# Moving 24 elementwise products from VectorE to GpSimd, decay rows to SyncE's queue, and v loads ahead of k, in a gated linear-attention and GEGLU kernel

## The chip, the cores and the metric

The kernel runs on one core of a Trainium2 chip. The metric is the device time of one execution in microseconds (us); lower is better. In the profiles PE is TensorE (PEld its weight loads), DVE is VectorE, ACT is ScalarE, POOL is GpSimd and SP is SyncE; "POOLq" and "SPq" are the queues on which GpSimd and SyncE issue DMA transfers. "L309" is line 309 of the kernel.

## The reference, cut to what matters

For 4 batches, 8 heads, 768 time steps and head size 48, a complex decay `a` is normalised, a state is decayed and updated at each step, and read out by q. The 3072 outputs of width 384 then pass through a gated feed-forward block.

```python
mag = np.sqrt(a_re * a_re + a_im * a_im)
scale = np.minimum(mag, 0.999) / (mag + 1e-06)
a_re_n, a_im_n = (a_re * scale, a_im * scale)
for t in range(S):                       # 768 steps
    new_re = ar * S_re - ai * S_im       # ar, ai: a_re_n, a_im_n at t
    new_im = ar * S_im + ai * S_re
    S_re, S_im = (new_re + k[t] v[t]^T, new_im)
    y[:, :, t] = q[t]^T S_re
...
gelu = 0.5 * g * (1.0 + erf(g * inv_sqrt2))        # g = x @ w_gate
ffn_out = gelu * val @ w_out                       # val = x @ w_val
out = x + ffn_out / (1.0 + np.exp(-(x @ w_res)))
```

## The kernel before

The kernel cuts the 768 steps into groups of 256 (12 groups in all; the tiles are 128 partitions by 768 columns: two blocks of 128 steps, each 8 heads of 48). The decay becomes cumulative sums of log-magnitude and angle. `E` and `Ei` are exp(+) and exp(-) of the first, `CS` holds cosine and sine of the second, and the attention works on `Q = q*E*CS` and `K = k*Ei*CS`. The products q*E and k*Ei are the subject of the change:

```python
def products(g):
    def x0():
        qE = pK.tile([128, W], BF, tag="qE", name="qE")
        nc.vector.tensor_tensor(out=qE, in0=flat(T["q", g]), in1=T["E", g], op=OP.mult)       # L309
        ...
    def x1():
        kE = pK.tile([128, W], BF, tag="kE", name="kE")
        nc.vector.tensor_tensor(out=kE, in0=flat(T["k", g]), in1=T["Ei", g], op=OP.mult)      # L314
        ...
    def mk(nm, src):                                      # Q from qE, K from kE:  L321
        ...  nc.vector.tensor_tensor(out=t, in0=T["CS", g], in1=sb, op=OP.mult)
    return [x0, mk("Q", "qE"), x1, mk("K", "kE")]
```

Other VectorE instructions that play a part below. The first two read two, respectively one, fp32 tile of SBUF (the engines' working memory), the third one int32 tile of SBUF:

```python
nc.vector.scalar_tensor_tensor(out=lm, in0=T["s", g], scalar=0.5, in1=lm, op0=OP.mult, op1=OP.add)   # L197
nc.vector.tensor_scalar(out=lm, in0=lm, scalar1=LNMAX, scalar2=None, op0=OP.min)                     # L198
...
nc.vector.tensor_scalar(out=fg[:, :, 0, :].bitcast(int32), in0=fg[:, :, 1, :].bitcast(int32), ...)   # L246
```

The decay of a whole group goes through DRAM as rows, to be turned into columns `m` and multiplied into `M` on VectorE (L282):

```python
def turn(nm, g, srcs):
    ...
    for i, src in enumerate(srcs):
        nc.gpsimd.dma_start(out=md[i:i + 1, :], in_=src)              # dm<-E, dm<-Ei, dm<-ar
    for u in range(2):
        nc.gpsimd.dma_start(out=m[u * D:(u + 1) * D]..., in_=md...)   # m<-dm
```

Each output block is stored twice: SyncE writes the gated part, then GpSimd adds x with an accumulating store, which has to wait until the first has landed (43.1 us in 13 waits of GpSimd in the kernel before). The v loads are on GpSimd's queue as well, each behind a one-element copy (`landed`) that waits for k's load (53.0 us in 8 waits):

```python
nc.sync.dma_start(out=out[t0:t0 + 128, :], in_=ot)                                                # L470
if u < NU - 1:
    nc.gpsimd.dma_start(out=out[t0:t0 + 128, :], in_=T["x", token(u, jj)], accum_op=OP.add)       # L472
...
for u in range(-1, NU + 1):
    phase_x(u)      # decay of unit u+1, output projection of unit u-1
    ...             # loads of the decays
    phase_y(u)      # gelu block of unit u, products and first attention of unit u+1
    for g in gs(u + 3):
        load_q(g)
        after_landing(T["k", g], call(load_v, g))
```

A unit is two groups but for the first and last. ACT's function table is loaded anew for logarithm and exponential, for arctangent and sine, and for gelu (21 loads of 1.28 us in the trace). That splits the execution: a load stage, then a decay stage and a gelu stage in turn, five times, then a tail. The table loads on ACT mark the borders: a decay stage runs from the load of the logarithm table to that of the gelu table. One more gelu stage stands at the end of the load stage and is counted with it. Stages are numbered below without it, but the expectations count it: their "second gelu stage" is the first of the five here.

Of the kernel before, what the change touches and what calls it, by code (L numbers as in the profile page):

```python
# [12 lines left out]
OP = mybir.AluOpType  # L13
# [3 lines left out]
def weave(*streams):  # L17

    order = []
    for si, (begin, end, steps) in enumerate(streams):  # L20
        n = len(steps)
        for i, step in enumerate(steps):
            order.append((begin + (end - begin) * (i + 0.5) / n, si, i, step))
    for _, _, _, step in sorted(order, key=lambda e: e[:3]):
        step()
# [3 lines left out]
def kernel(  # L29
# [13 lines left out]
    nc = tc.nc  # L43
    B, H, S, D = q.shape
# [47 lines left out]

    lda = ctx.enter_context(tc.tile_pool(name="lda", bufs=6))
    ldq = ctx.enter_context(tc.tile_pool(name="ldq", bufs=4))
    ldv = ctx.enter_context(tc.tile_pool(name="ldv", bufs=6))
    pS = ctx.enter_context(tc.tile_pool(name="pS", bufs=2))
    pE = ctx.enter_context(tc.tile_pool(name="pE", bufs=2))
    pQ = ctx.enter_context(tc.tile_pool(name="pQ", bufs=2))
    pK = ctx.enter_context(tc.tile_pool(name="pK", bufs=1))
    sqp = ctx.enter_context(tc.tile_pool(name="sqp", bufs=2))  # L100
    stt = ctx.enter_context(tc.tile_pool(name="stt", bufs=2))
    mp = ctx.enter_context(tc.tile_pool(name="mp", bufs=3))
    xp = ctx.enter_context(tc.tile_pool(name="xp", bufs=10))
    xtp = ctx.enter_context(tc.tile_pool(name="xtp", bufs=2))
    hb = ctx.enter_context(tc.tile_pool(name="hb", bufs=1))
    ob = ctx.enter_context(tc.tile_pool(name="ob", bufs=2))
# [7 lines left out]
    T = {}  # L114
# [11 lines left out]
    def rows(a, g, c):  # L126
        b, s = divmod(g, NS)
        t0 = (s * C + c) * 128
        return a[b, :, t0:t0 + 128, :].rearrange("h t d -> t h d")


    def load_a(g):
        for nm, src in (("ar", a_re), ("ai", a_im)):
            t = lda.tile([128, C, H, D], FP, tag=nm, name=nm)
            for c in range(C):
                nc.sync.dma_start(out=t[:, c], in_=rows(src, g, c))  # L136
            T[nm, g] = t
        T["a"] = g + 1

    def load_q(g):  # L140
        for nm, src in (("q", q), ("k", k)):
            t = ldq.tile([128, C, H, D], FP, tag=nm, name=nm)
            for c in range(C):
                nc.sync.dma_start(out=t[:, c], in_=rows(src, g, c))  # L144
            T[nm, g] = t

    def load_v(g):
        t = ldv.tile([128, C, H, D], BF, tag="v", name="v")
        for c in range(C):
            nc.gpsimd.dma_start(out=t[:, c], in_=rows(v, g, c))  # L150
        T["v", g] = t
# [16 lines left out]
    def after_landing(t, f):  # L168

        w = singles.tile([1, 1], FP, name="landed%d" % len(T))  # L170
        i = nc.gpsimd.tensor_copy(out=w, in_=t[0:1, C - 1, H - 1, D - 1:D])
        with tc.issue_after(i.ins):
            f()

    def flat(t):
        return t.rearrange("p c h d -> p (c h d)")
# [81 lines left out]
    def turn(nm, g, srcs):  # L258
        n = len(srcs)
        md = dr.tile([n, DM], FP, tag="d" + nm, name="d" + nm)  # L260
        for i, src in enumerate(srcs):
            nc.gpsimd.dma_start(out=md[i:i + 1, :], in_=src)
        m = mp.tile([128, n, H], FP, tag=nm, name=nm)
        for u in range(2):
            nc.gpsimd.dma_start(out=m[u * D:(u + 1) * D].rearrange("p r h -> p (r h)"),
                                in_=md.rearrange("r (h d) -> d (r h)", h=H))
        T[nm, g] = m

    def decay0(g):
        turn("m1", g, [T["lm", g][0:1, 0:DM]])  # L270
# [5 lines left out]
    def decay2(g):  # L276
        turn("m2", g, [T["E", g - 1][127:128, DM:W], T["Ei", g][0:1, 0:DM]])
# [28 lines left out]
    def products(g):  # L306
        def x0():
            qE = pK.tile([128, W], BF, tag="qE", name="qE")
            nc.vector.tensor_tensor(out=qE, in0=flat(T["q", g]), in1=T["E", g], op=OP.mult)  # L309
            T["qE", g] = qE  # L310

        def x1():
            kE = pK.tile([128, W], BF, tag="kE", name="kE")
            nc.vector.tensor_tensor(out=kE, in0=flat(T["k", g]), in1=T["Ei", g], op=OP.mult)  # L314
            T["kE", g] = kE

        def mk(nm, src):
            def x():
                t = pQ.tile([128, C * H, 2, D], BF, tag=nm, name=nm)
                sb = T[src, g].rearrange("p (x u d) -> p x u d", u=1, d=D).to_broadcast([128, C * H, 2, D])  # L320
                nc.vector.tensor_tensor(out=t, in0=T["CS", g], in1=sb, op=OP.mult)  # L321
                T[nm, g] = t
            return x
        return [x0, mk("Q", "qE"), x1, mk("K", "kE")]
# [150 lines left out]
    def table(nm):  # L475
        def f():
            tab(nc.scalar.preload_act_table_set(nm))  # L477
        return f

    def gs(u):  # L480
        return UNITS[u] if 0 <= u < NU else []
# [7 lines left out]
    def call(f, *a):  # L489
        return lambda: f(*a)  # L490
# [4 lines left out]
    def att_steps(u, half):  # L495

        todo = [(g, c, i * C + c) for i, g in enumerate(gs(u)) for c in range(C)]
        n = len(todo) // 2
        steps = []
        for i, (g, c, jj) in enumerate(todo[half * n:half * n + n]):  # L500
            steps += attention(g, c)
            if i > 0:
                steps.insert(-1, call(xt_step, u, jj - 1))
        if n:
            steps.append(call(xt_step, u, half * n + n - 1))
        return steps
# [50 lines left out]
    def phase_y(u):  # L557

        gv = []
        if 0 <= u < NU:  # L560
            table("gelu_and_others")()
            gv = [call(gv_step, u, f) for f in range(KF)]
            rp = [call(rp_step, u, jj) for jj in range(len(gs(u)) * C)]
            gv = gv[:8] + rp[:len(rp) // 2] + gv[8:] + rp[len(rp) // 2:]
        pr = [st for g in gs(u + 1) for st in products(g)]
        weave((0.0, 1.0, gv), (0.0, 0.4, pr), (0.3, 0.95, att_steps(u + 1, 0)))

    def load_first(g):
# [24 lines left out]
    for u in range(-1, NU + 1):  # L593
        phase_x(u)
        while u >= 0 and T["a"] < min(NG, gs(u + 1)[-1] + 6 if gs(u + 1) else NG):
            load_a(T["a"])
        phase_y(u)
        for g in gs(u + 3):
            load_q(g)
            after_landing(T["k", g], call(load_v, g))  # L600


# [28 lines left out]
```

## Time and profile before

Before the change the kernel takes 324.23 us (median of 3 runs, 323.4 to 324.4); the profiled execution spans 322.4 us. The stages, read from the table loads in ACT's timeline:

| stage | length (us) |
|---|---|
| load stage with its gelu stage | 83.5 |
| five decay stages | 17.9, 19.2, 19.6, 17.4, 12.0 (sum 86.1) |
| five gelu stages | 26.4, 26.0, 26.4, 26.3, 23.2 (sum 128.2) |
| tail | 24.6 |

Two lines of the page of the kernel before: busy us by engine (share of the span, instructions), and the chain of work that ended last, by engine:

```profile
PE 272.1 (84%) x2200; PEld 170.5 (53%) x2200; DVE 234.8 (73%) x431; ACT 209.8 (65%) x353; POOL 80.5 (25%) x115
...
PE 56%; SPq 12%; ACT 11%; DMA 9%; DVE 6%; issue 3%; POOL 1%; ACTq 0%; DVEq 0%; POOLq 0%
```

The view of busy time by window shows what a gelu stage is. Here is the fourth gelu stage of the kernel before (start and end, length, then busy time and count of PE, PEld, DVE, ACT, POOL; granted clock; DMA share; GB/s):

```profile
236.33:262.65 26.32, 26.32 (x271) 16.69 (x270) 22.54 (x40) 16.64 (x31) 1.73 (x2) 1.00 0.13 26
```

By the profile PE is busy for all of the 26.32 us: this gelu stage is as long as TensorE's work in it. A decay stage looks different. This is VectorE's timeline early in the second decay stage (127.8 to 147.0) of the kernel before (start, duration, instruction, count, and in brackets the idle time before it and what ended that):

```profile
132.32 1.83 DVE L189 TENSOR_TENSOR ai<-s,ai 128x768 f32<-128x768 f32 x2 [5.11 <-ACT s L124]
...
134.53 0.95 DVE L309 TENSOR_TENSOR qE<-q,E 128x768 bf16<-128x768 f32 x1
...
135.90 0.95 DVE L314 TENSOR_TENSOR kE<-k,Ei 128x768 bf16<-128x768 f32 x1
136.76 1.82 DVE L197 SCALAR_TENSOR_TENSOR ar<-s,ar 128x768 f32<-128x768 f32 x2
138.50 1.05 DVE L198 TENSOR_SCALAR ar<-ar 128x768 f32<-128x768 f32 x2
```

After a wait of 5.11 us for ACT, VectorE runs without a gap, and two products stand in that run. The waits of the kernel before (engine, line, what it waited for; us in total, times, longest), the two lines that the prediction leans on:

```profile
ACT CS L124 <- DVE fg L246: 20.7, 10, 5.2
...
DVE M L282 <- DMA m<-dm: 3.4, 3, 1.6
```

Finally the durations, in the groups of instructions with shapes kept apart (busy us, mean ns of one, idle before):

```profile
L309 DVE TENSOR_TENSOR qE<-q,E 128x768 bf16<-128x768 f32 x12 | 11.4, 950 | 6.8 <-DMA ar<-in_a_re_dram 3.5 <-ACT E L124 3.3
L314 DVE TENSOR_TENSOR kE<-k,Ei 128x768 bf16<-128x768 f32 x12 | 11.4, 946 | 0.0
L197 DVE SCALAR_TENSOR_TENSOR ar<-s,ar 128x768 f32<-128x768 f32 x12 | 11.3, 951 | 3.3 <-ACT s L124 3.3
L198 DVE TENSOR_SCALAR ar<-ar 128x768 f32<-128x768 f32 x12 | 7.0, 594 | 0.0
L246 DVE TENSOR_SCALAR fg<-fg 128x768 int32<-128x768 int32 x12 | 6.7, 558 | 0.0
```

The 24 products cost VectorE 22.8 us.

### The profile page before, as it was taken

To read this page: it belongs to the slowest core of one execution; us is meant where nothing else is said; L and a number is where in the kernel's file an instruction comes from. 1 tells how busy PE (TensorE), PEld (TensorE's weight loads), DVE (VectorE), ACT (ScalarE), POOL (GpSimd) and SP (SyncE) were. 2 spreads that over 40 slices of the span, in tenths; PEclk is the share of its full clock that TensorE was granted. 3 is DMA by queue.
4 is the path that set the end of the run, shared out by engine and by line. 5 is a ranking of instruction groups with operands and counts; after the bars stand their busy time and mean duration, and the time that the engine had idled before them with its cause. 6 is when DMAs were issued, how large, how long until landed. Compare 5 with 4: busy or idle time off the path is not lost.

```text
span 322.4 us, 5853 instructions
## 1 busy us (share of the span) xinstructions
PE 272.1 (84%) x2200; PEld 170.5 (53%) x2200; DVE 234.8 (73%) x431; ACT 209.8 (65%) x353; POOL 80.5 (25%) x115
## 2 busy tenths in 40 slices
PE   0337927789887999789997999998999999899994
PEld 0116624677543666445664556554656655555682
DVE  2446769968499995599982999974899837864352
ACT  4549684646998557977568976569665683656150
POOL 1206522022040370259020572000630003200220
PEclk9995676959999999999999999999999999999998
DMA  8999999989999995396850595000360003600441
GB/s 159 218 183 181 182 169 165 185 174 180 187 179 186 223 160 33 76 197 113 122 36 2 107 121 95 2 0 3 75 122 3 2 0 76 122 2 0 107 91 50
DMA packets 137755, 34.55 MB, mean 107 GB/s; under 512 B 126848, under 2 KB 137728, under 8 KB 137728
## 3 DMA queue, kind: packets, MB, share of 16 engines
q1 hardware_dynamic: 103296, 23.60, 36.8%
q0 software_dynamic: 34432, 10.59, 31.2%
q8 instruction: 17, 0.28, 0.3%
q14 instruction: 10, 0.08, 0.1%
HBM read 31.31 MB, written 9.07 MB: 125 GB/s over the span
## 4 chain that ended last, share of the span: by engine, by line
PE 56%; SPq 12%; ACT 11%; DMA 9%; DVE 6%; issue 3%; POOL 1%; ACTq 0%; DVEq 0%; POOLq 0%
PE vp L443 14%; PE gp L439 13%; SPq L136 6%; SPq L144 6%; PE op L463 6%; DMA k<-in_k_dram 4%; PE rp L455 3%; PE tp L349 3%; PE tp L346 3%; PE at L356 3%; ACT L477 3%; DMA m<-dm 3%; ACT s L124 3%; PE cst L236 2%; PE y L394 2%
## 5 line engine op out<-in xcount | busy, mean ns | idle before, releaser
L124 ACT ACTIVATE h<-gp 128x512 bf16<-128x512 f32 (+1 forms) x84 | 44.5, 536 | 38.4 <-PE gp L439 37.9
L439 PE MATMUL gp<-xT,wg 128*128 128x512 bf16 (+1 forms) x252 | 65.4, 353 | 3.4 <-ACT h L124 2.0
L443 PE MATMUL vp<-xT,wv 128*128 128x512 bf16 (+1 forms) x252 | 66.6, 353 | 0.0
L446 DVE SCALAR_TENSOR_TENSOR h<-h,vp 128x512 bf16<-128x512 bf16 (+1 forms) x84 | 49.8, 603 | 16.4 <-PE vp L443 12.0
L463 PE MATMUL op<-wo,h 128*128 128x384 bf16 x288 | 50.2, 326 | 8.1 <-ACT Ei L124 5.9
L463 PEld LDWEIGHTS <-h 128*128 128x128 bf16 x288 | 27.8, 98 | 28.7 <-issue 11.3
L351 ACT COPY qk<-tp 96x512 bf16<-96x512 bf16 x48 | 27.9, 580 | 17.1 <-PE tp L349 7.9
L359 DVE TENSOR_TENSOR atm<-at,mask 128x512 bf16<-128x512 f32 x48 | 32.9, 686 | 8.2 <-PE at L356 7.8
L472 POOL DMA_DIRECT2D out_dram<-x x22 | 20.4, 947 | 54.4 <-DMA out_dram<-ot 43.1
L439 PEld LDWEIGHTS <-wg 128*128 128x128 bf16 x252 | 23.7, 99 | 17.9 <-issue 4.2
L443 PEld LDWEIGHTS <-wv 128*128 128x128 bf16 x252 | 23.8, 99 | 13.3
L189 DVE TENSOR_TENSOR ai<-s,ai 128x768 f32<-128x768 f32 x12 | 11.1, 955 | 23.6 <-ACT s L124 23.6
L477 ACT ACT_TABLE_LOAD x21 | 26.9, 1283 | 1.1 <-PEq L615 0.7
L346 PE MATMUL tp<-ident,Q 128*96 128x128 bf16 x192 | 20.1, 231 | 6.9 <-DVE Q L321 6.2
L346 PEld LDWEIGHTS <-Q 128*96 128x96 bf16 x192 | 17.4, 130 | 15.3 <-DVE Q L321 10.0
L124 ACT ACTIVATE CS<-fg,hpi 128x768 bf16<-128x768 f32 x12 | 11.2, 935 | 20.8 <-DVE fg L246 20.7
L150 POOL DMA_DIRECT2D v<-in_v_dram x24 | 21.9, 932 | 4.2 <-DMA v<-in_v_dram 1.3
L349 PE MATMUL tp<-ident,K 128*96 128x128 bf16 x192 | 22.3, 235 | 0.0
L236 PE MATMUL cst<-ai,lt0b 128*128 128x384 f32 x24 | 11.8, 577 | 11.7 <-ACT ai L124 11.0
L352 DVE COPY qk<-tp 96x512 bf16<-96x512 bf16 x48 | 19.8, 413 | 2.3 <-ACT qk L351 1.7
L212 PE MATMUL csl<-ar,lt0a 128*128 128x384 f32 x24 | 11.4, 562 | 10.8 <-DMA ar<-in_a_re_dram 10.8
L466 DVE SCALAR_TENSOR_TENSOR ot<-sg,op 128x384 f32<-128x384 f32 x24 | 13.1, 547 | 10.1 <-PE op L463 10.1
(85 smaller groups left out, 522.0 us busy)
## 6 DMA issues: line engine op xcount, KB each, us to landing
ar<-in_a_re_dram SPq DMA_DIRECT2D x24, 192.0 KB, 4.7
ai<-in_a_im_dram SPq DMA_DIRECT2D x24, 192.0 KB, 4.1
q<-in_q_dram SPq DMA_DIRECT2D x24, 192.0 KB, 3.8
k<-in_k_dram SPq DMA_DIRECT2D x24, 192.0 KB, 3.7
out_dram<-ot SPq DMA_DIRECT2D x24, 192.0 KB, 2.5
out_dram<-x POOLq DMA_DIRECT2D x22, 192.0 KB, 3.7
v<-in_v_dram POOLq DMA_DIRECT2D x24, 96.0 KB, 5.0
wg<-in_moe_w_gate_dram POOLq DMA_DIRECT2D x4, 288.0 KB, 11.4
```

The costliest lines, as they stand in the source:

```text
L124: tab(nc.scalar.activation(**kw))
L150: nc.gpsimd.dma_start(out=t[:, c], in_=rows(v, g, c))
L346: nc.tensor.transpose(out=tp[0:DD, j * 128:j * 128 + 128], in_=Q(x), identity=ident)
L349: nc.tensor.transpose(out=tp[0:DD, 512 + j * 128:640 + j * 128], in_=K(x), identity=ident)
L351: nc.scalar.copy(out=qk[0:DD, 0:512], in_=tp[0:DD, 0:512])
L359: nc.vector.tensor_tensor(out=atm, in0=at, in1=mask4, op=OP.mult)
L439: nc.tensor.matmul(out=gp, lhsT=wg[:, fi, ffi * 128:(ffi + 1) * 128], rhs=xT[:, fi, :], start=(fi == 0), stop=(fi == KD - 1))
L443: nc.tensor.matmul(out=vp, lhsT=wv[:, fi, ffi * 128:(ffi + 1) * 128], rhs=xT[:, fi, :], start=(fi == 0), stop=(fi == KD - 1))
L446: nc.vector.scalar_tensor_tensor(out=h2[:, ffi, :], in0=h2[:, ffi, :], scalar=0.5, in1=vp, op0=OP.mult, op1=OP.mult)
L463: nc.tensor.matmul(out=ps, lhsT=h2[:, ffi, jj * 128:(jj + 1) * 128], rhs=wo[:, ffi, :], start=(ffi == 0), stop=(ffi == KF - 1))
L472: nc.gpsimd.dma_start(out=out[t0:t0 + 128, :], in_=T["x", token(u, jj)], accum_op=OP.add)
L477: tab(nc.scalar.preload_act_table_set(nm))
```

## The change

Its intent is to relieve VectorE by an engine that stands idle, to take the small row transfers off that engine's queue, and to let the v loads go ahead early. Of the diff, the sizes of two pools (`ldv` 6 to 5, `xp` 10 to 9, to make room) are left out:

```diff
-    pK = ctx.enter_context(tc.tile_pool(name="pK", bufs=1))
+    pK = ctx.enter_context(tc.tile_pool(name="pK", bufs=2))
 ...
-            nc.gpsimd.dma_start(out=md[i:i + 1, :], in_=src)
+            nc.sync.dma_start(out=md[i:i + 1, :], in_=src)
 ...
-            nc.gpsimd.dma_start(out=m[u * D:(u + 1) * D].rearrange("p r h -> p (r h)"),
+            nc.sync.dma_start(out=m[u * D:(u + 1) * D].rearrange("p r h -> p (r h)"),
 ...
-            nc.vector.tensor_tensor(out=qE, in0=flat(T["q", g]), in1=T["E", g], op=OP.mult)
+            nc.gpsimd.tensor_tensor(out=qE, in0=flat(T["q", g]), in1=T["E", g], op=OP.mult)
 ...
-            nc.vector.tensor_tensor(out=kE, in0=flat(T["k", g]), in1=T["Ei", g], op=OP.mult)
+            nc.gpsimd.tensor_tensor(out=kE, in0=flat(T["k", g]), in1=T["Ei", g], op=OP.mult)
 ...
-        pr = [st for g in gs(u + 1) for st in products(g)]
+        pr = [pp[i] for pp in [products(g) for g in gs(u + 1)] for i in (0, 2, 1, 3)]
 ...
+        if u > 0:
+            for g in gs(u + 2):
+                load_v(g)
         phase_y(u)
         for g in gs(u + 3):
             load_q(g)
-            after_landing(T["k", g], call(load_v, g))
+            if u < 0:
+                after_landing(T["k", g], call(load_v, g))
```

More of the change, by code (lines that the diff above doesn't have):

```diff
@@ L94 @@
     ldq = ctx.enter_context(tc.tile_pool(name="ldq", bufs=4))
-    ldv = ctx.enter_context(tc.tile_pool(name="ldv", bufs=6))
+    ldv = ctx.enter_context(tc.tile_pool(name="ldv", bufs=5))
     pS = ctx.enter_context(tc.tile_pool(name="pS", bufs=2))
@@ L102 @@
     mp = ctx.enter_context(tc.tile_pool(name="mp", bufs=3))
-    xp = ctx.enter_context(tc.tile_pool(name="xp", bufs=10))
+    xp = ctx.enter_context(tc.tile_pool(name="xp", bufs=9))
     xtp = ctx.enter_context(tc.tile_pool(name="xtp", bufs=2))
```

## The prediction

> **What bounds it now.** Busy: PE 84%, DVE 73%, ACT 65%, GpSimd 25%. To about 100 us the loads rule (DMA busy 0.8 to 0.99 in the slices). Then two stages alternate (busy by window):
> - Gelu stages (26 us each): PE 25.2 to 26.6 us busy, DVE 23. PE-bound.
> - Decay stages, windows 83-101, 128-147, 173-193, 219-236, 263-276 us: PE idles 1.1 to 3.8 us in each. In the VectorE timeline DVE first waits 3.6 to 5.1 us for ACT, then runs nearly unbroken to the end; ACT waits 0.7 to 3 us for the fractional-angle ops (fg) before the Sins. So their ends are DVE-bound; ACT could end 0.7, 2, 3, 4 and 6 us earlier.
>
> **What changes.**
> 1. 24 products (0.95 us each in the groups view, 22.8 us) leave DVE for GpSimd. One or two preceded fg in each decay stage. By instruction order qE and kE now start on GpSimd as soon as E and Ei exist, and Q, K, Q follow straight after the sines.
> 2. Twenty 0.78 us reads and fifteen 0.5 to 0.7 us writes of decay rows leave GpSimd's queue (24.6 us) for SyncE's. In the last three decay stages the chain of waits runs through them (3.2 us landing, plus queueing behind accumulating stores), and DVE stood 0.7, 1.0 and 1.6 us before M.
> 3. v loads precede the products and wait for no k.
>
> **Costs.** [...] GpSimd stays far from full. [...] SyncE will also hold its output stores while a row write lands. M now stands earlier in DVE's order and may still be waited for.
>
> **Sum on the critical path.** Decay stages: DVE relief plus shorter M wait 0.7+1.9+2.6+2.9+3.5, capped by PE's idle time in each (3.8, 3.3, 2.6, 2.0, 1.1): about 8 us. [...] Gelu stages stay PE-bound (0 to 1 us in total), the load stage gains 0 to 1 us. Net about 5.5 us: 324.2 to **318.5 us**, 80% range 310 to 326. Faster by over 2%: 0.43; within 2%: 0.48; slower by over 2%: 0.09.
>
> **What would show it.** Right: DVE busy near 212 us; [...] decay stages 1 to 2 us shorter, gelu stages unchanged at 26 us; ACT's wait for fg before Sin falls from 20.7 us towards 10; PE's wait for Q falls; single DVE ops stretch where a product runs. Wrong: decay stages equal in length, with DVE stretched or waiting for kE or M; or gelu stages shortening too, which would mean PE busy hid DVE waits.
>
> **What would make it wrong.** [...] products far over 2 us, so that Q and K wait for them; row reads on SyncE queued behind big loads; or PE's record overstating its load, so that relief of DVE pays in full (312 or less).

The sum was about 8 us for the decay stages, less 3 us for VectorE being held up by GpSimd's products, plus 0 to 1 us each from the gelu stages and the load stage, put at about 5.5 us net: from 324.2 to 318.5 us. That SyncE holds output stores while a row write lands, the changed kernel shows once: an `ot` was ready at 102.36 us, and its store went out at 116.01, after SyncE had waited 1.5 us for `dm<-ar` to land.

## The result, and the profile after

The changed kernel takes 343.91 us (median of 4 runs, 341.36 to 345.91), against 323.88 us for the kernel before in the same rounds: ratio 1.0617, 95% interval 1.056 to 1.0673. It is slower by 6%, and the prediction's range (310 to 326) does not hold it. Ratios here and below are the mean time of one kernel's fast runs over that of the other's of the same rounds, so they are not quite the ratio of the medians quoted beside them.

| stage (us) | before | after |
|---|---|---|
| load stage with its gelu stage | 83.5 | 84.9 |
| decay stages | 17.9, 19.2, 19.6, 17.4, 12.0 | 19.6, 20.7, 22.5, 17.7, 11.4 |
| gelu stages | 26.4, 26.0, 26.4, 26.3, 23.2 | 37.0, 26.3, 29.2, 27.1, 23.1 |
| tail | 24.6 | 24.5 |

Of the 21.8 us that the span grew, 10.6 lie in one gelu stage, 5.9 in the decay stages, and most of the rest in the third and fourth gelu stage. The same lines of the page as before, for the changed kernel:

```profile
PE 276.6 (80%) x2177; PEld 173.4 (50%) x2200; DVE 228.2 (66%) x407; ACT 210.0 (61%) x353; POOL 104.4 (30%) x97
...
PE 55%; DVE 14%; ACT 9%; SPq 8%; DMA 7%; issue 5%; POOL 1%; DVEq 0%; ACTq 0%; POOLq 0%
```

VectorE lost 24 instructions worth 22.8 us, but its busy time fell by 6.6 us only, and its share of the chain rose from 6% to 14%. So its other instructions took longer: the durations add up to 12.2 us more, and busy time counts overlapping instructions once, so the two figures don't add up exactly. The groups of the changed kernel say which:

```profile
L309 POOL TENSOR_TENSOR qE<-q,E 128x768 bf16<-128x768 f32 x12 | 29.6, 2464 | 89.8 <-ACT E L124 89.7
L314 POOL TENSOR_TENSOR kE<-k,Ei 128x768 bf16<-128x768 f32 x12 | 22.9, 1910 | 0.0
...
L197 DVE SCALAR_TENSOR_TENSOR ar<-s,ar 128x768 f32<-128x768 f32 x12 | 15.0, 1259 | 3.4 <-ACT s L124 3.3
L246 DVE TENSOR_SCALAR fg<-fg 128x768 int32<-128x768 int32 x12 | 10.1, 840 | 0.1
L198 DVE TENSOR_SCALAR ar<-ar 128x768 f32<-128x768 f32 x12 | 8.8, 740 | 0.0
```

The three groups L197, L246 and L198 together grew from 25.0 to 33.9 us. (The two ai multiplies of a unit, L189, kept their 0.95 us.) The waits of the changed kernel, to be set against 20.7 us for the first of them before, and none for the second:

```profile
ACT CS L124 <- DVE fg L246: 29.8, 11, 6.7
...
DVE K L321 <- POOL kE L314: 8.5, 1, 8.5
```

The second line is one wait of 8.5 us, and it lies in the long gelu stage (104.6 to 141.6). TensorE stood for want of it, from 108.5 to 116.8 us, and its mean granted clock in that stage was 0.86, against 1.00 in the same stage before. The clock was 0.50 from 112.2 to 122.4 us, so TensorE also worked more slowly for 5.6 us after its wait (four L346 matmuls took 0.63 us at 119.67 and 0.39 at 123.10); how much of the 10.6 us is due to that, no run separates. Here is GpSimd's timeline of the changed kernel around it, columns as before:

```profile
90.94 2.35 POOL L309 TENSOR_TENSOR qE<-q,E 128x768 bf16<-128x768 f32 x1 [3.69 <-ACT E L124]
93.25 1.81 POOL L314 TENSOR_TENSOR kE<-k,Ei 128x768 bf16<-128x768 f32 x1
95.04 2.52 POOL L309 TENSOR_TENSOR qE<-q,E 128x768 bf16<-128x768 f32 x1
112.53 0.95 POOL L472 DMA_DIRECT2D out_dram<-x  x1 [14.98 <-DMA out_dram<-ot]
113.19 2.12 POOL L314 TENSOR_TENSOR kE<-k,Ei 128x768 bf16<-128x768 f32 x1
```

GpSimd took these in the order of its queue: the kE began at 113.19 us, after the store at 112.53. Between the unit's last qE and its last kE stands an accumulating store, and that store waits 14.98 us until the first store of the same block has landed. SyncE's timeline tells why that was late, first the changed kernel:

```profile
102.79 4.13 SPq L136 DMA_DIRECT2D ar<-in_a_re_dram  x4
107.02 0.94 SPq L144 DMA_DIRECT2D q<-in_q_dram  x1
108.06 0.92 SPq L470 DMA_DIRECT2D out_dram<-ot  x1
```

and the same store in SyncE's timeline of the kernel before:

```profile
95.28 6.56 SPq L136 DMA_DIRECT2D ar<-in_a_re_dram  x4
101.95 0.64 SPq L470 DMA_DIRECT2D out_dram<-ot  x1
```

In the changed kernel VectorE began that `ot` at 91.52 us and had it by 92.07; SyncE issued its store at 108.06, behind loads. Before, it went out at 101.95, and nothing on GpSimd that VectorE needed stood behind it. In VectorE's timeline of the changed kernel the two effects show as two stretched instructions and one long wait:

```profile
94.36 1.53 DVE L197 SCALAR_TENSOR_TENSOR ar<-s,ar 128x768 f32<-128x768 f32 x1
95.81 2.16 DVE L246 TENSOR_SCALAR fg<-fg 128x768 int32<-128x768 int32 x1
...
115.35 0.96 DVE L321 TENSOR_TENSOR K<-CS,kE 128x1536 bf16<-128x1536 bf16 x1 [8.46 <-POOL kE L314]
```

The stretched L246 (2.16 us against 0.56) ran while GpSimd made the qE that began at 95.04.

### The profile page after: what moved, and what is told of

The parts are those of the page before. It is cut to its first block, busy times and chain, and to the rows that moved or that the text cites. A ratio compares the mean times of both kernels' runs of the same rounds, so it can differ in the third digit from the quotient of the medians.

```text
span 344.2 us, 5885 instructions
## 1 busy us (share of the span) xinstructions
PE 276.6 (80%) x2177; PEld 173.4 (50%) x2200; DVE 228.2 (66%) x407; ACT 210.0 (61%) x353; POOL 104.4 (30%) x97
## 4 chain that ended last, share of the span: by engine, by line
PE 55%; DVE 14%; ACT 9%; SPq 8%; DMA 7%; issue 5%; POOL 1%; DVEq 0%; ACTq 0%; POOLq 0%
PE vp L443 13%; PE gp L439 12%; PE op L463 6%; SPq L136 5%; PE tp L346 4%; PE tp L349 3%; DMA ai<-in_a_im_dram 3%; PE rp L455 3%; PE at L356 3%; ACT s L124 3%; DVE ar L197 3%; PE y L394 2%; DMA m<-dm 2%; PE dk L386 2%; DVE r L243 2%
## 5 line engine op out<-in xcount | busy, mean ns | idle before, releaser
L439 PE MATMUL gp<-xT,wg 128*128 128x512 bf16 (+1 forms) x236 | 63.0, 353 | 5.4 <-DVE xT L430 3.7
L443 PE MATMUL vp<-xT,wv 128*128 128x512 bf16 (+1 forms) x245 | 65.3, 356 | 0.9 <-DVE fg L244 0.5
L446 DVE SCALAR_TENSOR_TENSOR h<-h,vp 128x512 bf16<-128x512 bf16 (+1 forms) x84 | 50.4, 606 | 23.0 <-PE vp L443 17.1
L463 PE MATMUL op<-wo,h 128*128 128x384 bf16 x288 | 52.6, 336 | 12.5 <-ACT Ei L124 6.4
L309 POOL TENSOR_TENSOR qE<-q,E 128x768 bf16<-128x768 f32 x12 | 29.6, 2464 | 89.8 <-ACT E L124 89.7
L351 ACT COPY qk<-tp 96x512 bf16<-96x512 bf16 x48 | 27.9, 580 | 37.2 <-PE tp L349 27.6
L463 PEld LDWEIGHTS <-h 128*128 128x128 bf16 x288 | 28.5, 100 | 34.8 <-issue 13.3
L472 POOL DMA_DIRECT2D out_dram<-x x22 | 19.5, 914 | 74.0 <-DMA out_dram<-ot 72.6
L150 POOL DMA_DIRECT2D v<-in_v_dram x24 | 22.0, 926 | 37.4 <-PE y L396 17.9
L443 PEld LDWEIGHTS <-wv 128*128 128x128 bf16 x252 | 24.1, 100 | 16.9 <-issue 1.6
L124 ACT ACTIVATE CS<-fg,hpi 128x768 bf16<-128x768 f32 x12 | 11.2, 934 | 29.8 <-DVE fg L246 29.8
L189 DVE TENSOR_TENSOR ai<-s,ai 128x768 f32<-128x768 f32 x12 | 11.1, 954 | 26.4 <-ACT s L124 20.4
L346 PE MATMUL tp<-ident,Q 128*96 128x128 bf16 x192 | 20.4, 233 | 6.8 <-DVE Q L321 6.1
L346 PEld LDWEIGHTS <-Q 128*96 128x96 bf16 x192 | 17.7, 132 | 14.4 <-DVE Q L321 9.4
L386 PE MATMUL dk<-v,K 128*96 128x48 bf16 x160 | 14.1, 211 | 11.7 <-DVE G L370 8.4
L314 POOL TENSOR_TENSOR kE<-k,Ei 128x768 bf16<-128x768 f32 x12 | 22.9, 1910 | 0.0
```

The lines of the kernel that those rows point to most:

```text
L124: tab(nc.scalar.activation(**kw))
L309: nc.gpsimd.tensor_tensor(out=qE, in0=flat(T["q", g]), in1=T["E", g], op=OP.mult)
L314: nc.gpsimd.tensor_tensor(out=kE, in0=flat(T["k", g]), in1=T["Ei", g], op=OP.mult)
L346: nc.tensor.transpose(out=tp[0:DD, j * 128:j * 128 + 128], in_=Q(x), identity=ident)
L351: nc.scalar.copy(out=qk[0:DD, 0:512], in_=tp[0:DD, 0:512])
L439: nc.tensor.matmul(out=gp, lhsT=wg[:, fi, ffi * 128:(ffi + 1) * 128], rhs=xT[:, fi, :], start=(fi == 0), stop=(fi == KD - 1))
```

## The experiments

Theory A: some of VectorE's instructions (L197, L198 and L246 above) take longer while GpSimd makes products, by far more than the 3 us that the forecast took off, and one product is caught behind a DMA in GpSimd's queue; the relief of VectorE is worth little. Theory B: the moved transfers (rows on SyncE, early v loads) are the cause. A third question is what the relief alone is worth.

Two measures serve all runs. The stage lengths are taken from the table loads, as above. The *stretch* is the time by which VectorE's instructions in a stage exceed the median duration of the same form in the kernel before, summed over those at least 0.15 us longer. Only what VectorE's instructions lost is in it, not what other engines then waited. In the table, "start" is the load stage with its gelu stage. It is paced by loads (the page's DMA row is 8 or 9 tenths in every slice of it, before and after) and varies by up to some 3 us between executions (84.8 us in e1, 87.9 in e9) for reasons that no run settled, so small differences are read from the decay and gelu columns.

| run (profiled execution) | start | decay sum | stretch in it | gelu sum | tail |
|---|---|---|---|---|---|
| before | 83.5 | 86.1 | 0.3 | 128.2 | 24.6 |
| after | 84.9 | 92.0 | 10.4 | 142.8 | 24.5 |
| e1_rest_only | 84.8 | 84.6 | 0.0 | 126.9 | 24.5 |
| e2_products_only | 88.2 | 111.9 | 24.4 | 132.5 | 24.2 |
| e3_acc_behind_products | 91.0 | 93.0 | 11.5 | 130.7 | 24.5 |
| e4_dummy_products | 85.1 | 112.3 | 23.3 | 131.0 | 24.6 |
| e5_fill_instead | 83.4 | 88.2 | 3.2 | 130.0 | 24.3 |
| e6_no_products | 82.9 | 93.9 | 0.0 | 129.8 | 24.5 |
| e7_rows_on_sync_only | 83.8 | 83.9 | 0.0 | 128.4 | 24.5 |
| e8_second_group_on_gpsimd | 99.9 | 83.8 | 1.4 | 134.8 | 24.5 |
| e9_relief_alone | 87.9 | 82.4 | 0.0 | 129.5 | 24.5 |
| e10_second_group_first_in_queue | 85.0 | 83.8 | 1.4 | 133.6 | 24.5 |
| e11_products_in_quarters | 85.1 | 85.4 | 4.4 | 129.1 | 24.4 |
| e12_late_v | 90.0 | 92.7 | 11.2 | 131.8 | 24.5 |

### The two halves of the change

The change without its products (the diff is against the changed kernel):

```diff
-            nc.gpsimd.tensor_tensor(out=qE, ...)      # and kE
+            nc.vector.tensor_tensor(out=qE, ...)      # and kE
```

> The changed kernel with the 24 products put back on VectorE; decay rows on SyncE's queue, early v loads and pool sizes stay. Theory A (the loss comes from the products on GpSimd: kE of the second group stuck behind an accumulating store in GpSimd's queue, 8.5 us of VectorE waiting in the second gelu stage[...]): 319 to 326 us, no VectorE wait for kE, L197 and L246 back at 0.95 and 0.56 us. Theory B (the loss comes from the decay rows on SyncE or from the early v loads in the load stage): 335 us or more.

Measured: 322.58 us, ratio 0.9958 (0.9934 to 0.9983). This is as theory A expected. Theory B falls: the moved transfers alone make the kernel a little faster.

The products alone (against the kernel before, with the changed order and the changed pool sizes):

```diff
-            nc.vector.tensor_tensor(out=qE, ...)      # and kE
+            nc.gpsimd.tensor_tensor(out=qE, ...)      # and kE
```

> The kernel before with the products on GpSimd alone (their order and the pool sizes of the changed kernel with them). Theory A: 332 to 342 us, with VectorE waiting for kE in the second gelu stage, but less than 8.5 us if the early v loads are what pushed the first output store from 102 to 108 us on SyncE's queue. Theory B: 321 to 326 us.

Measured: 357.43 us, ratio 1.1029 (1.0996 to 1.1063): worse than the whole change, and 15 us above what theory A had expected. VectorE never waited for a kE here, so nothing of the loss comes from a product caught in the queue as in the changed kernel. In the first decay stage of this run VectorE shows one instruction that takes 5.17 us instead of 0.95:

```profile
97.60 5.17 DVE L197 SCALAR_TENSOR_TENSOR ar<-s,ar 128x768 f32<-128x768 f32 x1
102.69 0.55 DVE L246 TENSOR_SCALAR fg<-fg 128x768 int32<-128x768 int32 x1
```

and GpSimd's timeline of the same run has three products one behind the other over just that time:

```profile
96.58 1.84 POOL L309 TENSOR_TENSOR qE<-q,E 128x768 bf16<-128x768 f32 x1
98.37 1.81 POOL L314 TENSOR_TENSOR kE<-k,Ei 128x768 bf16<-128x768 f32 x1
100.14 1.81 POOL L309 TENSOR_TENSOR qE<-q,E 128x768 bf16<-128x768 f32 x1
```

VectorE waited, as it seems, through the rest of the first product and through two more, which followed without a gap: L197 ended 0.82 us after the last of them, about its own duration. The L197 group went from 11.3 to 26.0 us, L198 from 7.0 to 15.2. The stretch explains the decay stages nearly one for one. In the first four, the stretch is 6.5, 6.1, 6.4 and 5.4 us, and the stages are 6.0, 6.6, 6.9 and 4.3 us longer than before. The whole change shows the same against e1, which differs from it in the products alone: stretch 2.2, 2.1, 4.1, 2.1, growth 2.0, 1.3, 3.4, 1.2. A companion of the stretch is not separated from it: TensorE's mean granted clock in these four stages was 0.86, 0.87, 0.87 and 0.92 in e2, and 1.00 in the kernel before.

That the products alone do more harm than the whole change is not fully settled. In e2 the row transfers and `landed` copies stand in GpSimd's queue too, and by the traces the products begin at other moments (96.58 us here, 90.94 in the changed kernel); a train of three then meets L197.

### Is it the products, or that GpSimd is busy?

"Port" is the word for the supposition that VectorE and GpSimd hold each other up by the tiles that they read or write, not by GpSimd being occupied. No run shows what in the chip does it, only which instructions took longer, and beside what. In the kernel before, with all its own products left on VectorE, each product was also made a second time by GpSimd into a tile that nobody reads:

```diff
+            d = pD.tile([128, W], BF, tag="dum", name="dumq")      # and dumk
+            nc.gpsimd.tensor_tensor(out=d, in0=flat(T["q", g]), in1=T["E", g], op=OP.mult)
```

> The kernel before, plus a second copy of each product on GpSimd into a scratch tile that nobody reads; VectorE keeps its own. No instruction waits for the copies except loads into q and k buffers and GpSimd's own DMA issues. Theory A (port): [...] each decay stage grows 1 to 3 us, total 327 to 334 us. If the port costs nothing: 323 to 325 us, no op stretched.

Measured: 361.34 us (354.82 to 362.45). Three of the four runs are more than 1.5% above the fastest, so no ratio is given; the profiled one is the fastest. Even that one is far above the expectation. The line of this run that matches L197 elsewhere (11.3 us before; the added lines shift the numbers by one):

```profile
L198 DVE SCALAR_TENSOR_TENSOR ar<-s,ar 128x768 f32<-128x768 f32 x12 | 20.4, 1707 | 3.3 <-ACT s L125 3.3
```

Nothing waits for the results of these products, yet the decay stages grow by 26 us and the stretch in them is 23.3 us. So no wait for the products' results is needed to explain it. But loads and DMA issues stand behind them in GpSimd's queue, so its mere occupation was still a rival.

Then GpSimd was kept as busy at the same places with work that reads one element only (`fill` is called with E or Ei after each of VectorE's products):

```diff
+    def fill(src):
+        d = pD.tile([128, W], BF, tag="dum", name="dum")
+        nc.gpsimd.tensor_copy(out=d[0:1, 0:1], in_=src[0:1, W - 1:W])
+        for _ in range(3):
+            nc.gpsimd.memset(d, 0.0)
```

> The kernel before, plus GpSimd work at the same places as in the run with copies of the products, but work that reads almost nothing from SBUF: a one-element copy that waits for E or Ei, then three fills of a scratch tile of the products' size. Port theory: ops with two SBUF inputs (L189, L197, L309, L314) keep their 0.95 us[...], total 323 to 330 us. Rival (merely keeping GpSimd and its queue busy costs the time, through late decay rows, v loads and accumulating stores): 345 us or more, like the copies' 361.

Measured: 328.41 us, ratio 1.0119 (1.0061 to 1.0176), GpSimd busy 139.2 us (130.4 in e4, 104.4 in the changed kernel). That is within the expectation, and the rival's 345 us or more is refuted. The groups of this run, where the added lines shift all numbers by one or more (L198 here is L197 elsewhere, L199 is L198, L247 is L246):

```profile
L198 DVE SCALAR_TENSOR_TENSOR ar<-s,ar 128x768 f32<-128x768 f32 x12 | 11.3, 951 | 3.3 <-ACT s L125 3.3
L247 DVE TENSOR_SCALAR fg<-fg 128x768 int32<-128x768 int32 x12 | 8.6, 718 | 0.0
L199 DVE TENSOR_SCALAR ar<-ar 128x768 f32<-128x768 f32 x12 | 8.2, 692 | 0.0
```

The two-input instructions keep 0.95 us (L198 here 951 ns; the ai multiplies 954, qE 950 and kE 947). Only the one-input ones stretch, which treat the same 768 columns in 0.55 us when undisturbed: L247 from 558 to 718 ns on average, L199 from 594 to 692. So it matters what GpSimd does: L197 averages 0.95 us against memsets, which read no tile, and 2.17 us against products (e2). The fills are shorter than the products (0.82 us on average), but that is not what spared L197: six of the twelve ran beside a fill for 0.37 to 0.91 us and none took more than 0.96, while products cut to 0.58 us stretched it to 1.34 (next experiment).

### Shorter products

The same products on GpSimd, each cut into four instructions of 192 columns. To keep the queue block out of the way this run also has the accumulating stores behind the products, as the next experiment does:

```diff
-            nc.gpsimd.tensor_tensor(out=qE, in0=flat(T["q", g]), in1=T["E", g], op=OP.mult)
+            for p in range(4):
+                ps = slice(p * W // 4, (p + 1) * W // 4)
+                nc.gpsimd.tensor_tensor(out=qE[:, ps], in0=flat(T["q", g])[:, ps], in1=T["E", g][:, ps], op=OP.mult)
```

> The changed kernel with accumulating stores behind the products (339 us), each product cut into four instructions of 192 columns. If the port is handed over after every GpSimd instruction: no VectorE op is held longer than about 0.6 us, total 326 to 333 us. If VectorE waits until GpSimd has nothing left to start: single ops still stretch by 2 to 5 us, total 337 us or more.

Measured: 327.69 us, ratio 1.0127 (1.0073 to 1.0181), as expected if GpSimd and VectorE take turns after every instruction. The groups of this run:

```profile
L197 DVE SCALAR_TENSOR_TENSOR ar<-s,ar 128x768 f32<-128x768 f32 x12 | 12.9, 1081 | 4.0 <-ACT s L124 3.9
L198 DVE TENSOR_SCALAR ar<-ar 128x768 f32<-128x768 f32 x12 | 7.7, 647 | 0.0
```

The longest L198 takes 0.94 us here, against 5.84 us in the next experiment, which differs only in the uncut products. No VectorE instruction lost more than 0.40 us, and the whole stretch is 6.1 us against 20.0. The same work on the same engine, handed over in smaller pieces, costs 11.4 us less (10 to 11 us if each run is set against the kernel before of its own rounds), although GpSimd itself works longer: four pieces of 0.58 us for a product of 1.80. So in these runs VectorE paid for the length of the GpSimd instructions, and with pieces of 0.58 us a wait was no longer carried through a train of them (0.40 us lost at most).

### The product caught in GpSimd's queue

The changed kernel with the accumulating stores collected and issued behind the unit's last kE:

```diff
-            nc.gpsimd.dma_start(out=out[t0:t0 + 128, :], in_=T["x", token(u, jj)], accum_op=OP.add)
+            T.setdefault("acc", []).append((t0, T["x", token(u, jj)]))
 ...
+            with tc.issue_after(T["last"].ins):        # the unit's last kE
+                for t0, x in todo:
+                    nc.gpsimd.dma_start(out=out[t0:t0 + 128, :], in_=x, accum_op=OP.add)
```

> The changed kernel with every accumulating store put behind the products of its unit in GpSimd's queue. Theory A: the 8.5 us wait for kE goes, the second gelu stage returns from 37 to about 26 us, and the time falls by 8 to 11 us to 332 to 336 us; the stretched VectorE ops stay. If the port alone is the cause: no change, 341 us or more.

Measured: 339.08 us, ratio 1.0446 (1.0406 to 1.0486). The long gelu stage falls from 37.0 to 25.8 us, as it should if the store caused it. The total gains 4.8 us only, 3 us short of the expectation, because the start took 6 us more: one L198 of the load stage was stretched beside a train of products. VectorE's timeline of this run:

```profile
52.99 5.84 DVE L198 TENSOR_SCALAR ar<-ar 128x768 f32<-128x768 f32 x1
```

The other way to the same end is to let the store go out earlier. The changed kernel with the v loads as before:

```diff
-        if u > 0:
-            for g in gs(u + 2):
-                load_v(g)
 ...
-            if u < 0:
-                after_landing(T["k", g], call(load_v, g))
+            after_landing(T["k", g], call(load_v, g))
```

> The changed kernel with one part undone: the v loads wait for k and are issued after the y stage's work, as before; products stay on GpSimd, decay rows stay on SyncE. In the changed kernel the first output store left SyncE at 108.1 us instead of 102.0, and the accumulating store on GpSimd, which waits for it, held back a kE so that VectorE waited 8.5 us for it and the second gelu stage took 37.0 us. Theory A (the early v loads are what makes that store late): the wait falls to about 2.5 us, the stage to 28 to 30 us, the total to 333 to 340 us; the decay stages stay stretched (sum 90 to 94 us). Rival (the store is late because the products on GpSimd make everything ahead of it late, whatever the v loads do): the wait stays above 6 us and the total at 342 us or more.

Measured: 341.17 us, ratio 1.0573 (1.0509 to 1.0637). The store left SyncE at 101.85 us, the kE behind it started at 105.97, VectorE's wait for it is gone, and the stage took 25.8 us. So the early v loads made the store late, and theory A holds on that; by what path loads on GpSimd's queue held up SyncE's was not traced. The stage did better than expected and the total worse, 1 us outside the expectation, and VectorE's timeline of this run shows why:

```profile
49.32 7.21 DVE L198 TENSOR_SCALAR ar<-ar 128x768 f32<-128x768 f32 x1
```

GpSimd's timeline of the same run:

```profile
49.00 1.83 POOL L309 TENSOR_TENSOR qE<-q,E 128x768 bf16<-128x768 f32 x1
50.77 1.83 POOL L314 TENSOR_TENSOR kE<-k,Ei 128x768 bf16<-128x768 f32 x1
52.53 1.82 POOL L309 TENSOR_TENSOR qE<-q,E 128x768 bf16<-128x768 f32 x1
54.29 1.81 POOL L314 TENSOR_TENSOR kE<-k,Ei 128x768 bf16<-128x768 f32 x1
```

An instruction of 0.55 us began just after the first of four products and ended when the last was done. That this stretch was spared the changed kernel is luck of timing: there the same four products began at 51.87 us instead of 49.00, because the copy and the wo loads ahead of them in GpSimd's queue came later. There they met mostly L243 and L244, which read `cst` from PSUM (where TensorE's L236 had left it) and kept their 0.55 us, and the start of the changed kernel is 5 us shorter. What stays in decay and gelu stages is mainly the stretch (11.2 us): 224.5 us together, 13 more than in e1 (211.5).

### What the relief is worth

The change with each product cut to 8 columns on VectorE, so that its 22.8 us are gone and GpSimd is left alone (Q and K are made from constant tiles of which these 8 columns are rewritten; the result is wrong):

```diff
-            nc.gpsimd.tensor_tensor(out=qE, in0=flat(T["q", g]), in1=T["E", g], op=OP.mult)
+            nc.vector.tensor_tensor(out=qE[:, 0:8], in0=flat(T["q", g])[:, W - 8:W], in1=T["E", g][:, W - 8:W], op=OP.mult)
```

> The run without GpSimd products (322.6 us), but each product on VectorE shrunk to 8 of its 768 columns, so that 22 us leave VectorE, nothing goes to GpSimd, and loads and scheduling keep all their waits on the products: wrong result on purpose. It repeats the run without products, which was spoiled by one 12.2 us wait for the decay rows. If the prediction's relief term is right: 314 to 316 us. If the decay stages gain less than 1 us each and the gelu stages give it back, as the undisturbed stages of that run suggest: 319 to 322 us.

Measured: 323.38 us (321.63 to 326.16), ratio 0.9977 (0.9939 to 1.0014), against 0.9958 for e1, which keeps the products on VectorE. That is 1 us above the expectation for a worthless relief and 7 above that for the predicted one: the relief is worth nothing that can be measured. The decay stages are 2.2 us shorter than in e1, the gelu stages 2.6 us longer. In the fourth gelu stage the view by window shows the exchange, e9 first:

```profile
237.61:264.76 27.15, 26.93 (x271) 16.80 (x276) 21.27 (x38) 17.25 (x30) 1.70 (x2) 1.00 0.13 26
```

and e1:

```profile
235.31:261.39 26.08, 25.84 (x266) 16.50 (x269) 22.20 (x41) 16.91 (x30) 1.70 (x2) 1.00 0.13 24
```

PE nearly fills both stages. With the shorter decay stage ahead of it, seven more weight loads (276 against 269) fall into the gelu stage, and PE needs 1.1 us more there. TensorE's work that used to hide in the decay stage is done later instead. Over the five gelu stages it is 1257 weight loads against 1249, and PE is busy 1.4 us more (126.0 against 124.6); in the decay stages it is busy 1.2 us less (72.2 against 73.3). So this accounts for about half of the 2.6 us; the rest is idle time of TensorE that was not traced. All this is from two profiled executions.

An earlier try took the changed kernel and left the products out altogether, with a constant tile in their place (wrong result):

```diff
-            qE = pK.tile([128, W], BF, tag="qE", name="qE")
-            nc.gpsimd.tensor_tensor(out=qE, in0=flat(T["q", g]), in1=T["E", g], op=OP.mult)
-            T["qE", g] = qE
+            T["qE", g] = fixed          # and kE
```

> The changed kernel with the 24 products left out altogether, Q and K made from a constant tile: wrong result on purpose. It shows what taking 22.8 us off VectorE is worth when GpSimd costs nothing. If the prediction's relief term was right (8 us in the decay stages, gelu stages unchanged): 312 to 316 us against 322.6 with the products on VectorE and all else equal. If VectorE's load did not set the ends of the decay stages: 319 us or more.

Measured: 334.68 us, ratio 1.0308 (1.0247 to 1.0368), in the range for a worthless relief, but by accident. This run says nothing of the relief, because q and k were no longer read, and nothing held back the loads into their buffers. SyncE issued q, k and ar loads from 135.05 to 141.2 us and only then, at 141.30, the row write of Ei. VectorE waited 12.2 us once for m, and the second decay stage took 31.0 us. It does show a hazard of the rows on SyncE that the changed kernel does not meet.

### Parts that might be kept

Only the rows on SyncE (against the kernel before):

```diff
-            nc.gpsimd.dma_start(out=md[i:i + 1, :], in_=src)       # and the two reads back
+            nc.sync.dma_start(out=md[i:i + 1, :], in_=src)
```

> The kernel before with the decay rows on SyncE's queue as the only change. The early v loads seemed to delay the load stage by 1.3 us in the run without GpSimd products (322.6 us), so this should give 320 to 323 us, with shorter waits of VectorE for M (3.4 us before). If the row moves are worth nothing: 323.5 to 324.5 us.

Measured, with five rounds: 321.92 us against 324.52, ratio 0.9909 (0.9862 to 0.9957). This is as expected, and the fastest version measured: 0.9% better than the kernel before, a gain clear of noise. Three of the eleven runs of the kernel before in these rounds lay near 327.5 us; without them the gain is 0.7%. VectorE's wait for m is 1.1 us instead of 3.4, and ACT's wait for fg is 18.8 us instead of 20.7.

Adding the products of every second group on GpSimd, with the thought that those are less pressing:

```diff
+        eng = nc.gpsimd if g > 0 and g % 2 == 0 else nc.vector
 ...
-            nc.vector.tensor_tensor(out=qE, ...)      # and kE
+            eng.tensor_tensor(out=qE, ...)            # and kE
```

> As e7, but the products of the second group of each pair are made on GpSimd, gated by the single qE and kE buffers so that they start only once VectorE has made Q and K of the first group, that is at the start of the gelu stage, where nearly all VectorE operands come from PSUM. Port theory: hardly any stretched op, 319 to 324 us, if no accumulating store blocks them. If products on GpSimd hurt wherever they stand: 328 us or more.

Measured: 344.45 us, ratio 1.0606 (1.0555 to 1.0658), far above the 319 to 324 us hoped for. It is the queue again. GpSimd's timeline of this run:

```profile
69.99 0.17 POOL L171 COPY landed<-k 1x1 f32<-1x1 f32 x1 [16.90 <-DMA k<-in_k_dram]
...
75.09 0.17 POOL L171 COPY landed<-k 1x1 f32<-1x1 f32 x1 [3.12 <-DMA k<-in_k_dram]
...
77.08 1.82 POOL L311 TENSOR_TENSOR qE<-q,E 128x768 bf16<-128x768 f32 x1
```

A product stands behind two one-element copies that wait for the k of a later group. VectorE waited 14.7 us for this qE, and the gelu stage at the end of the load stage took 35.7 us instead of 18.9 (e7). With products, then stores and v loads, in that order:

```diff
+            with tc.issue_after(T["last"].ins):       # the unit's last product on GpSimd
+                ...                                   # accumulating stores; later the v loads
```

> As the run with only the second group's products on GpSimd (344.5 us), but accumulating stores and v loads of a unit stand behind its products in GpSimd's queue. Theory: that run lost its time to products stuck behind instructions that wait for a transfer (14.7 us at one place), not to the port; so this gives 319 to 325 us and hardly any VectorE wait for GpSimd. If it is the port or the length of the products: 335 us or more.

Measured: 328.93 us, ratio 1.0155 (1.0121 to 1.019). The expectation is missed. The queue block is gone (VectorE's wait for qE is 2.0 us), but the version is slower than e7, and the loss is in the gelu stages: 27.5, 27.9, 27.2 and 28.0 us, 0.8 to 1.8 us more than in e7. The products now meet other instructions: in the second and third gelu stage one cast of `Gb` (L379) each took 1.6 and 1.0 us longer. That is 2.6 us, half of the growth of the gelu stages of 5.3 us over e7; the other half stays unexplained. (The Q group took 13.0 us instead of 11.4 by one instruction at 63.7 us, in the stage before these.)

## Why the prediction was wrong, point by point

Three terms of its sum failed: the relief (about 8 us predicted, nothing measurable found), the hold-up of VectorE (3 us, against a stretch of 12.2 us) and the gelu stages (0 to 1 us, against 14.6).

- "DVE relief plus shorter M wait ... about 8 us." This is the step that failed first. The relief alone is worth nothing measurable (e9 against e1: 0.9977 and 0.9958 of the kernel before). The prediction let ACT end 0.7, 2, 3, 4 and 6 us earlier in the five decay stages, which is about the time for which it stands idle in each (0.7, 2.1, 2.5, 3.9 and 5.6 us in the kernel before), as if all of it were VectorE's doing. With the products gone (e9) ACT still stands idle for 0.3, 1.3, 1.4, 2.8 and 5.5 us, and the stages get only 2.2 us shorter in all, because other engines fill them: in the first three ACT's own chain of table loads and functions is busy 17.2 of 17.5, 16.9 of 18.2 and 17.1 of 18.5 us, and in the fifth TensorE is busy 11.9 of 12.0. What holds the fourth was not traced. And the gelu stages get 2.6 us longer, about half of it TensorE's work that no longer hides in the decay stages.
- The 3 us taken off for VectorE being held up. That VectorE's instructions take longer beside products was foreseen, and the runs show it; the size was wrong. The stretch measured is 12.2 us in the changed kernel (10.4 in the decay stages, 1.9 ahead of them), and 2.2, 2.1, 4.1, 2.1 and 0 us in the five decay stages. In the changed kernel no single instruction lost more than 2.2 us. In e2 and e12 products in trains held one for 5.17 and 7.21 us in all, a size that the prediction did not consider.
- "Gelu stages stay PE-bound (0 to 1 us in total)." They grew by 14.6 us. The largest part, 10.6 us, comes from one kE behind an accumulating store in GpSimd's queue. The prediction had the pieces apart (accumulating stores on GpSimd's queue, output stores on SyncE that are held up) and did not join them: work that another engine waits for was put into a queue with instructions that wait for DMAs. e3 and e12 both bring that stage back to 25.8 us.
- The third and fourth gelu stage, 29.2 and 27.1 us, are filled by PE too (28.84 and 26.84 us busy); the third holds 1.67 us of the output projection (L463), which in the kernel before had ended in the decay stage. The stretch delays TensorE in a decay stage, and part of that work slides into the next stage. The granted clock has a share in it: it was 0.50 from 204.5 to 211.1 us, at the end of the third decay stage, and twelve L463 matmuls took 4.02 us there against 2.11 us a little earlier in the stage.
- The time of a product on GpSimd: 1.80 us measured when nothing stands in its way, against 0.95 on VectorE. In the changed kernel qE averages 2.46 us, which fits GpSimd waiting for VectorE too: three that began 0.28 us after an L189 took 2.35 us each.
- "DVE busy near 212 us": 228.2, since the stretch counts as busy. "ACT's wait for fg before Sin falls from 20.7 us towards 10": it rose to 29.8, for fg comes from L246, and L197 and L198 stand ahead of it in VectorE's queue. "PE's wait for Q falls": 9.4 us instead of 10.0, nothing to speak of.
- "What would make it wrong" had the ai multiplies that ACT waits for held up. Those (L189) kept their 0.95 us; ACT waited longer all the same, by way of L197, L198 and L246. It named products far over 2 us, so that Q and K wait for them; K did wait, 8.5 us, but for a product of 2.12 us that stood in a queue. It also named rows behind big loads; in the changed kernel this did not happen (VectorE waited 0.6 us for m in all), though e6 shows it can (12.2 us at once).
- The rest of the change, for which the prediction gives no separate figure, does no harm: e1 measured 0.9958, e7 0.9909.

Open remain: why e2 stretches twice as much as the whole change does, beyond the shifted moments that the traces show; the share of TensorE's lower granted clock; half of the gelu growth in e10; and the variation of the start between executions.

## What to carry to other kernels

An idle GpSimd was no free VectorE here: before moving an elementwise instruction there, list what VectorE runs at the same moments. The instructions that lost most here read SBUF tiles alone (L197 went from 951 to 2170 ns in e2, L198 from 594 to 1274), while L243 and L244, which read PSUM, kept their 0.55 us. What was lost was not a share of a GpSimd instruction but up to a whole train of them (7.21 us for an instruction of 0.55 us in e12); short pieces (here 192 columns) limited the loss to 0.40 us. Never put a result that another engine waits for behind an instruction that waits for a DMA in the same queue: here the store waited 14.98 us, and VectorE 8.5 us for the kE behind it. And where two kinds of stage alternate, price a relief by cutting the work out altogether (with a wrong result) before building the move: here it would have shown that there was nothing to win (0.9977 of the time before in e9, 0.9958 in e1).
